# S5 scan and GEGLU on one core: later loads on GpSimd's queue, the fourth token tile after the up weights

## The chip, the cores and the metric

The kernel runs on one core of one Trainium2 chip. The metric is device time in microseconds (us), the median of several executions. Engines are named as in the profile: PE (TensorE, matrix products), PEld (its weight loads), DVE (VectorE), ACT (ScalarE), POOL (GpSimd), SP (SyncE). An engine with a small q (SPq) is its instruction queue; on SP the queue does nothing but issue transfers.

## The reference, cut to what matters

Two branches share a layer norm without weights. Branch A is a diagonal complex state-space scan over 2048 tokens; branch B is a gated feed-forward block.

```python
xn = layernorm(x)                                   # x: 1 x 2048 x 512
# A: P = 512 complex states
dt = exp(log_dt); Lam_bar = exp(dt * Lam)
Bu = einsum("bld,pd->blp", xn, ((Lam_bar - 1) / Lam)[:, None] * Bmat)
for t in range(L): h = Lam_bar * h + Bu[:, t]
s = 2 * einsum("blp,dp->bld", hs, Cmat).real + xn * Dskip
# B: F = 1376
g = silu((gelu(xn @ w_gate) * (xn @ w_up)) @ w_down)
out = x + s * g
```

Inputs and output are bf16.

## The kernel before, in words

The 2048 tokens are worked off in four **slabs** of 512, each slab in four tiles of 128 tokens (tokens on the partitions). `x_tok` holds all tokens. For each slab:

- **norm** (L721 on): statistics of the tokens; for slab 1 on DVE with `bn_stats` (L274), for slabs 2 and 3 on ACT (L738), then the reciprocal root on POOL (L732, L755), and normalised tokens in `xna` on ACT (L743). `dma_t4` (L355) is a transposing DMA from `xna` to `xnT`.
- **B product** (`half`, L528): PE multiplies `xnT` with `BT`, ACT empties the PSUM banks into `U` (L530). DVE turns `U` by a table of angles (`tab`, L540, L548 and L552), runs a real scan per 128 states (L559), and turns back, which gives the states `hst`.
- **gate** (`gate_tile`, L433): the up and gate products in three column chunks of 512, 512 and 352; ACT empties them (L436, Gelu for the gate), DVE multiplies them into `at` (L442, L444). `at_t` (L449) is a transposing DMA from `at` to `atT`, one per tile.
- **down** (`down_pair`, L465): eleven matmuls `atT` by `wd` per tile, Silu on ACT (L468).
- **y** (`y_tile`, L481): states by `C2`; the bank is seeded by ACT with the skip term `sk` (L477), which DVE makes from `xna` and `Drow` (`skip`, L360). DVE multiplies by Silu (L486), adds `x` (L491), and SP stores the tile (L494).

`C2` comes from `CT`, the transposed C matrices. `CT` is the tile `hst1` under another name: two transposing DMAs (L706) write it, ACT multiplies it (L708), DVE combines it (L710, L713), and the second slab's states overwrite it later.

**Slab 0 is special**, since weights are still arriving. Tokens are only centred, not scaled, at first (`center`: sum on ACT L342, subtraction on DVE L343), transposed on PE (`head_t`, L323, copied out by DVE L325), and the root of the variance is put in when the banks are emptied (L391, L407). `squares` (L347, ACT) and `rstd` (L281 to L284, POOL) give that root. `up_rows` (L382) takes the up weight in four row tiles as they land: each row tile is multiplied for token tiles 0 and 1 into six PSUM banks. `first_w` (L401) does the rest of the up products and all gate products of slab 0 with whole columns. PSUM has six `ring` banks and two `ybank` banks.

**Order of work.** Every step is recorded with its engine, and the instructions are emitted in the order of the list `ORDER`, a permutation written out by hand from a planner's run; what the calls give the planner (costs, `rank`, `after`, `not_before`, landing times) is not used when the program is built; only the data steps read and write, and `ORDER`, count. Each engine runs its instructions in that order, and waits only for the data and buffers of its own steps. So an instruction that waits holds all that stand behind it on its engine.

**Queues.** All loads but three tiny ones are issued by SP, in this order: x tiles 0 and 1, up row 0, x tile 2, up row 1, x tile 3, up rows 2 and 3, the gate weight in one (L219, L211), the two B matrices (transposing, L231), slab 0's `xnT` (L355), slab 1's tokens (L214), `wd` without its last 96 rows (L668), Dskip's row to all partitions (L232), then the `atT` transposes, the rest of `wd` (L670), slab 2's tokens, slab 1's `xnT`, the two C matrices (L706), slab 3's tokens. A step on SP waits also for an earlier transfer that used the same completion counter. POOL issues no transfer.

Of the kernel before, what the change touches and what calls it, by code (L numbers as in the profile page):

```python
# [21 lines left out]
    13, 14, 24, 16, 15, 17, 19, 18, 25, 12, 0, 20, 21, 1, 22, 2, 23, 3, 4, 27, 26, 5, 39, 6, 28, 7, 29, 30, 33, 40, 59, 32, 34, 31, 60, 35, 41, 62, 8,  # L22
    61, 48, 63, 9, 67, 36, 42, 49, 56, 43, 44, 37, 65, 64, 45, 68, 50, 51, 66, 57, 52, 69, 70, 47, 46, 10, 71, 54, 72, 82, 58, 53, 136, 138, 74, 55,
    80, 76, 140, 142, 124, 144, 86, 73, 75, 125, 128, 126, 38, 84, 127, 81, 88, 85, 129, 92, 205, 83, 79, 130, 189, 96, 87, 90, 97, 100, 94, 99, 132,
    149, 91, 112, 89, 11, 104, 210, 95, 102, 212, 105, 110, 93, 103, 120, 101, 77, 78, 206, 98, 118, 108, 145, 208, 207, 209, 107, 211, 213, 106, 214,
    113, 116, 109, 146, 155, 117, 215, 137, 151, 115, 139, 143, 150, 157, 119, 111, 121, 122, 123, 141, 153, 158, 219, 131, 148, 154, 170, 172, 217,
    176, 152, 267, 216, 174, 114, 133, 218, 227, 156, 220, 225, 177, 173, 171, 344, 228, 175, 147, 231, 221, 159, 224, 160, 191, 271, 161, 164, 165,
    162, 190, 233, 350, 273, 192, 239, 272, 275, 234, 410, 222, 163, 223, 167, 232, 226, 269, 270, 268, 235, 254, 229, 236, 240, 230, 252, 168, 256,
    193, 169, 166, 178, 255, 253, 257, 237, 250, 290, 286, 251, 194, 195, 238, 274, 284, 288, 179, 276, 180, 277, 287, 291, 292, 294, 305, 301, 183,
    196, 285, 295, 278, 181, 289, 299, 197, 293, 302, 198, 303, 184, 316, 307, 300, 304, 306, 297, 296, 182, 199, 317, 308, 320, 314, 309, 280, 200,  # L30
    201, 321, 186, 310, 315, 322, 318, 202, 282, 323, 203, 187, 319, 324, 335, 329, 279, 325, 281, 312, 188, 204, 331, 337, 333, 326, 185, 327, 134,
    298, 283, 345, 339, 311, 334, 330, 351, 349, 346, 313, 328, 356, 135, 357, 352, 332, 347, 368, 336, 362, 369, 340, 370, 372, 241, 338, 371, 415,
    242, 389, 341, 358, 353, 373, 416, 385, 391, 402, 363, 374, 245, 243, 386, 413, 246, 244, 406, 387, 247, 342, 248, 343, 348, 354, 392, 403, 411,
    375, 407, 457, 412, 417, 249, 258, 388, 404, 429, 408, 431, 430, 418, 390, 414, 405, 259, 263, 261, 419, 435, 444, 409, 260, 359, 420, 432, 262,
    437, 433, 265, 438, 434, 436, 445, 452, 427, 446, 453, 428, 447, 440, 421, 439, 448, 442, 467, 450, 367, 364, 449, 478, 451, 361, 266, 422, 473,
    465, 443, 376, 466, 474, 424, 355, 471, 458, 479, 463, 469, 486, 494, 454, 455, 377, 365, 423, 472, 468, 425, 264, 470, 426, 360, 464, 476, 488,
    490, 456, 495, 487, 381, 484, 492, 489, 491, 475, 366, 477, 480, 459, 485, 499, 379, 380, 496, 515, 517, 481, 378, 500, 482, 493, 497, 460, 382,
    501, 383, 498, 441, 461, 527, 513, 529, 511, 516, 611, 528, 518, 530, 505, 483, 384, 512, 514, 393, 394, 545, 397, 510, 396, 531, 543, 549, 533,
    546, 532, 544, 534, 398, 395, 400, 550, 547, 401, 548, 561, 506, 519, 507, 555, 559, 553, 551, 560, 562, 552, 520, 502, 503, 554, 399, 574, 612,
    522, 557, 576, 566, 556, 613, 558, 614, 521, 577, 575, 567, 568, 570, 508, 579, 563, 509, 581, 569, 571, 582, 616, 524, 583, 572, 617, 573, 523,  # L40
    564, 578, 618, 525, 565, 580, 587, 585, 596, 591, 589, 588, 626, 526, 586, 592, 535, 584, 590, 597, 627, 598, 604, 606, 593, 536, 599, 607, 605,
    621, 602, 600, 540, 594, 622, 633, 631, 601, 595, 615, 619, 603, 537, 608, 609, 620, 610, 539, 462, 623, 538, 634, 541, 635, 636, 628, 542, 624,
    637, 639, 504, 629, 638, 644, 632, 625, 630, 640, 645, 641, 642, 649, 659, 654, 643, 650, 646, 647, 648, 660, 651, 655, 652, 661, 653, 662, 656,
    663, 657, 658,
# [36 lines left out]
def kernel(  # L81
# [17 lines left out]
    nc = tc.nc  # L99
# [113 lines left out]
    def load_slab(s, put, issue, land, **kw):  # L213
        put(issue, land, lambda: nc.sync.dma_start(out=x_tok[:, s * M : (s + 1) * M, :], in_=x_r[:, s * M : (s + 1) * M, :]),  # L214
            writes=[("x", s, m) for m in range(M)], **kw)
# [6 lines left out]
    load_x(1, 1.59, 3.35)  # L222
    load_w("wu", 0, 1, 2.06, 4.6)
    load_x(2, 2.53, 4.95)
    load_w("wu", 1, 2, 3.0, 6.1)
    load_x(3, 3.5, 6.45)
    load_w("wu", 2, 3, 4.0, 7.6)
    load_w("wu", 3, 4, 5.0, 8.8)
    load_w("wg", 0, KT, 6.0, 12.8)
    for ri, src in enumerate((A_B_re, A_B_im)):  # L230
        dma_sp((9.0, 11.5)[ri], (15.3, 17.8)[ri], lambda ri=ri, src=src: nc.sync.dma_start_transpose(out=BT[:, ri, :, :], in_=src), [("BT", ri)])  # L231
    dma(SP, 1.4, 4.9, lambda: nc.sync.dma_start(out=Drow[:], in_=A_Dskip.partition_broadcast(P)), writes=["Drow"], after=list(sp_last))  # L232
# [44 lines left out]
    def rstd(m0, m1):  # L277

        def f():
            if m0 == 0:  # L280
                G.tensor_scalar(out=ve[:, 0:1], in0=mv[:, 0, 1:2], scalar1=EPS, scalar2=None, op0=ALU.add)  # L281
            else:
                G.tensor_scalar(out=ve[:, m0:m1], in0=ss[:, m0:m1], scalar1=1.0 / D, scalar2=EPS, op0=ALU.mult, op1=ALU.add)
            G.tensor_tensor(out=rs[:, 0, m0:m1], in0=ve[:, m0:m1], in1=mhalf[:, m0:m1], op=ALU.pow)  # L284
        pool(0.65 + 0.2 * (m1 - m0), f, [("mv", 0) if m == 0 else ("ss", m) for m in range(m0, m1)] + ["mhalf"], [("rs", 0, m) for m in range(m0, m1)],
             rank=250.0 - 20 * m0)
# [13 lines left out]
    def head_t(m):  # L300
# [17 lines left out]
        bank, key = (ybank[0], ("y", 0)) if m == 1 else (ring[7 - m], ("bank", 7 - m))  # L318
# [27 lines left out]
    def squares(m):  # L346
        acts(512, lambda: act(out=junk()[:], in_=x_tok[:, m, :], func=AF.Square, bias=ma[:, m : m + 1], accum_out=ss[:, m : m + 1]), [("x", 0, m), ("ma", m)], [("ss", m)],  # L347
             ptr=2, rank=150.0 - 10 * m, after=sums0)
# [5 lines left out]
    def dma_t4(s):  # L354
        dma(SP, 2.9 if s < 2 else 1.75, 3.5 if s == 0 else 2.7, lambda: nc.sync.dma_start_transpose(  # L355
            out=xnT[:, s % 2].rearrange("p m k t -> p (m k) t"), in_=xna[:].rearrange("p m d -> p (m d)")),
            [("xn", m) for m in range(M)], [("xnT", s % 2, m) for m in range(M)], rank=20.0)
# [6 lines left out]
    ring_n = [4]  # L364
# [8 lines left out]
    def up_rows(m, k):  # L373

        bs = (0, 1, 2) if m == 0 else ("y0", "y1", 3)
        ps = [ybank[int(r[1])] if isinstance(r, str) else ring[r] for r in bs]
        keys = [("y", int(r[1])) if isinstance(r, str) else ("bank", r) for r in bs]
        ups[m] = list(zip(ps, keys))

        def f():  # L380
            for (a, b), t in zip(CH, ps):
                T.matmul(t[:, 0 : b - a], lhsT=xcT[:, k, m * P : (m + 1) * P], rhs=wu[:, k, a:b], start=(k == 0), stop=(k == KT - 1))  # L382
        pe(3, F // 3, f, [("xcT", m, k // 2), ("wu", k)], keys)
        if k == KT - 1:
            for c in range(3):
                out_up(m, c, *ups[m][c])
# [68 lines left out]
    def down_pair(s, h):  # L455
        gi = g2_n[0] % NG2
        g2_n[0] += 1
        for b in range(2):
# [7 lines left out]
            pe(NFT, 512, f, [("atT", m), "wd"], [("bank", r)])  # L466
# [175 lines left out]
    rstd(1, 2)  # L642
    rstd(2, M)
# [8 lines left out]
    up_rows(1, 2)  # L652
    head_t(3)
    up_rows(0, 3)
    up_rows(1, 3)
    for m in range(2, M):
        for c in range(3):
            first_w("wu", m, c)
    for m in range(M):
        first_gates(m)  # L660
    tables()
# [3 lines left out]
    dma_t4(0)  # L665
    for m in range(M):
        at_t(0, m)
    dma(SP, 0.6, 6.7, lambda: nc.sync.dma_start(out=wd[:, 0 : NFT - 1, :], in_=B_w_down[0 : (NFT - 1) * P, :].rearrange("(k p) d -> p k d", p=P)),  # L668
        reads=[("xnT", 0, 0)], writes=["wd0"], after=list(sp_last))
    dma(SP, 0.5, 4.0, lambda: nc.sync.dma_start(out=wd[:FL, NFT - 1, :], in_=B_w_down[(NFT - 1) * P : F, :]), reads=["wd0"], writes=["wd"])  # L670
# [34 lines left out]
    for ri, src in enumerate((A_C_re, A_C_im)):  # L705
        dma(SP, 2.6, 2.6, lambda ri=ri, src=src: nc.sync.dma_start_transpose(out=CT[:, ri, :, :], in_=src), reads=["wd"], writes=[("CT", ri)])  # L706
# [15 lines left out]
    def norm(s):  # L722
        if s > 1:
            load_slab(s, lambda i, l, e, **kw: dma(SP, i, l, e, **kw), 0.55, 4.0, not_before=30.0)
        else:
            load_slab(1, lambda i, l, e, **kw: dma(SP, i, l, e, after=sp_last[:1], **kw), 0.55, 4.0)
# [93 lines left out]
```

## Time and profile before

| what | value |
|---|---|
| median of 3 runs | 181.9 us (181.57 to 182.25) |
| the profiled execution's own time | 181.37 us |
| its span, first to last instruction | 179.6 us |
| PE busy | 172.4 us, 835 matmuls in the record |
| DVE busy | 155.0 us |
| ACT busy | 126.2 us |
| POOL busy | 11.2 us |
| granted TensorE clock | 1.000 |
| HBM read, written | 6.46 MB, 2.10 MB |

A matmul's end is modelled in the profile, so successive rows overlap; pace is read from start to start. In a timeline a row gives start, length, engine, line, operation, output and inputs, how many were merged, and in brackets how long the engine had been idle and what released it. In the chain of waits a "DMA" piece is the time from a transfer's issue to its landing. "DMA share" is the mean busy share of the core's 16 DMA engines; it can pass 1 where packets overlap.

### The profile page before, as it was taken

The numbers are of one execution on the slowest core, as the hardware profiler recorded it, in microseconds if no ns is written. First come the engines' busy times: TensorE is split into PE (matmuls) and PEld (weight loads), VectorE is DVE, ScalarE is ACT, GpSimd is POOL, SyncE is SP. The second block draws the span as 40 slices with busy tenths as digits, with TensorE's granted clock in tenths as the row PEclk, the third lists the DMA queues.
The fourth block names the chain that finished last, engine by engine and source line by source line (L and its number), as shares of the span: only waits on it lengthen the run. The fifth ranks groups of instructions, "written<-read, shape, count | busy, mean of one in ns | idle before, by whom it ended". The sixth has DMA issues, their size and how long they took to land.

```text
span 179.6 us, 2405 instructions
## 1 busy us (share of the span) xinstructions
PE 172.4 (96%) x835; PEld 82.5 (46%) x850; DVE 155.0 (86%) x252; ACT 126.2 (70%) x240; POOL 11.2 (6%) x23
## 2 busy tenths in 40 slices
PE   7889998999999999999999999999999999999992
PEld 2445543444445554444445544444445445544451
DVE  3658387999999996899999996999999989999663
ACT  5688968999899999995678695658136665561530
POOL 2460003000011000000003000000000000000000
PEclk9999999999999999999999999999999999999999
DMA  5999989899300406900500007973000009045111
GB/s 160 321 295 237 249 276 185 197 220 234 97 0 0 80 0 132 150 0 6 133 0 5 0 0 148 190 148 75 0 0 0 29 30 153 10 98 121 57 61 59
DMA packets 46979, 18.66 MB, mean 104 GB/s; under 512 B 40216, under 2 KB 45944, under 8 KB 46968
## 3 DMA queue, kind: packets, MB, share of 16 engines
q1 hardware_dynamic: 46944, 18.52, 46.6%
q8 instruction: 6, 0.10, 0.2%
q14 instruction: 5, 0.04, 0.1%
q10 hardware_dynamic: 24, 0.00, 0.0%
HBM read 6.46 MB, written 2.10 MB: 48 GB/s over the span
## 4 chain that ended last, share of the span: by engine, by line
PE 81%; DMA 8%; DVE 6%; ACT 2%; issue 1%; SPq 1%; ACTq 0%; DVEq 0%
PE ring L433 31%; PE ring L465 21%; PE ybank L481 14%; PE ring L528 14%; DMA wu<-in_B_w_up_dram 5%; DMA x_tok<-in_A_x_dram 3%; DVE st L274 1%; ACT gt L407 1%; ACT at L391 1%; DVE yg L486 1%; DVE Q L620 1%; DVE tab L620 1%; DVE at L415 1%; DVE ot L491 1%; SPq L219 0%
## 5 line engine op out<-in xcount | busy, mean ns | idle before, releaser
L433 PEld LDWEIGHTS <-xnT 128*128 128x128 bf16 x288 | 28.2, 98 | 28.4
L465 PE MATMUL ring<-wd,atT 128*128 128x512 bf16 (+1 forms) x171 | 39.4, 379 | 0.3
L433 PE MATMUL ring<-wg,xnT 128*128 128x512 bf16 (+1 forms) x142 | 31.5, 356 | 0.1
L433 PE MATMUL ring<-wu,xnT 128*128 128x512 bf16 (+1 forms) x140 | 31.1, 356 | 0.2
L528 PE MATMUL ring<-xnT,BT 128*128 128x512 bf16 x128 | 29.7, 379 | 1.0 <-ACT gt L407 0.8
L559 DVE TENSOR_TENSOR_SCAN Fs<-rho,ini,W 128x512 bf16<-128x512 f32 x24 | 29.9, 1273 | 0.1
L481 PE MATMUL ybank<-C,hst 128*128 128x512 bf16 x118 | 27.4, 379 | 0.1
L465 PEld LDWEIGHTS <-atT 128*128 128x128 bf16 (+1 forms) x176 | 17.2, 98 | 20.8
L436 ACT ACTIVATE gt<-ring 128x512 bf16<-128x512 f32 (+1 forms) x36 | 19.7, 560 | 9.2 <-PE ring L433 9.0
L436 ACT ACTIVATE ub<-ring 128x512 bf16<-128x512 f32 (+1 forms) x36 | 19.1, 559 | 7.8 <-PE ring L433 7.7
L530 ACT ACTIVATE U<-ring 128x512 bf16<-128x512 f32 x32 | 18.1, 598 | 4.9 <-PE ring L528 4.7
L528 PEld LDWEIGHTS <-BT 128*128 128x128 bf16 x128 | 12.5, 98 | 16.5 <-issue 1.8
L481 PEld LDWEIGHTS <-hst 128*128 128x128 bf16 x136 | 13.3, 98 | 13.9
L540 DVE TENSOR_TENSOR Q<-U,tab 128x4096 bf16<-128x4096 bf16 x8 | 18.3, 2290 | 0.3
L540 DVE TENSOR_TENSOR Q<-Fs,tab 128x4096 bf16<-128x4096 bf16 x8 | 18.3, 2286 | 0.1
L468 ACT ACTIVATE g<-ring 128x512 f32<-128x512 f32 x16 | 9.3, 597 | 12.8 <-PE ring L465 12.8
L486 DVE TENSOR_TENSOR yg<-ybank,g 128x512 bf16<-128x512 f32 x15 | 10.2, 686 | 5.4 <-PE ybank L481 3.6
L477 ACT ACTIVATE ybank<-sk 128x512 f32<-128x512 bf16 x15 | 9.0, 601 | 4.4 <-DVE yg L486 4.4
L401 PEld LDWEIGHTS <-W 128*128 128x128 bf16 x72 | 7.0, 98 | 6.8
L442 DVE TENSOR_TENSOR at<-gt,ub 128x1024 bf16<-128x1024 bf16 x12 | 8.2, 683 | 2.2 <-ACT ub L436 1.5
L738 ACT ACTIVATE junk<-x_tok 128x512 bf16<-128x512 bf16 x16 | 10.0, 630 | 0.0
L743 ACT ACTIVATE xna<-x_tok,nb,rs 128x512 bf16<-128x512 bf16 x12 | 9.8, 833 | 0.0
(128 smaller groups left out, 174.1 us busy)
## 6 DMA issues: line engine op xcount, KB each, us to landing
out_dram<-ot SPq DMA_DIRECT2D x15, 128.0 KB, 1.9
x_tok<-in_A_x_dram SPq DMA_DIRECT2D x3, 512.0 KB, 5.1
wu<-in_B_w_up_dram SPq DMA_DIRECT2D x4, 344.0 KB, 4.3
wg<-in_B_w_gate_dram SPq DMA_DIRECT2D x1, 1376.0 KB
wd<-in_B_w_down_dram SPq DMA_DIRECT2D x1, 1280.0 KB, 7.8
x_tok<-in_A_x_dram SPq DMA_DIRECT2D x4, 128.0 KB, 2.6
atT<-at SPq DMA_TRANSPOSE x16, 3.7
Drow<-in_A_Dskip_dram SPq DMA_DIRECT2D x1, 128.0 KB, 7.5
```

The costliest lines, as they stand in the source:

```text
L433: T.matmul(ps[:, 0 : b - a], lhsT=xnT[:, s % 2, m, k, :], rhs=wt[:, k, a:b], start=(k == 0), stop=(k == KT - 1))
L436: acts(b - a, lambda: act(out=dst[:, a:b], in_=ps[:, 0 : b - a], func=AF.Copy if up else AF.Gelu_apprx_tanh), [("bank", r)], [key], table= ...
L465: T.matmul(ps[:], lhsT=atT[:fs, k, m * P : (m + 1) * P], rhs=wd[:fs, k, :], start=(k == 0), stop=(k == NFT - 1))
L468: acts(512, lambda b=b, ps=ps: act(out=g2[gi][:, b, :], in_=ps[:], func=AF.Silu), [("bank", r)], [("g2", gi, b)], table="silu", rank=3.0)
L481: T.matmul(ps, lhsT=hst[s % 2][:, j // NPT, j % NPT, m * P : (m + 1) * P], rhs=C2[:, j // NPT, j % NPT, c0:c1], start=(j == 0 and not seed ...
L486: dve(w, lambda: V.tensor_tensor(out=yg[e][:, c0:c1], in0=ps, in1=g2[gi][:, b, c0:c1], op=ALU.mult), [key, ("g2", gi, b)], [("yg", e, c0)])
L528: T.matmul(ps[:], lhsT=BT[:, ri, k, pt * P : (pt + 1) * P], rhs=xnT[:, s % 2, :, k, :], start=(k == 0), stop=(k == KT - 1))
L530: acts(512, lambda q=q, ri=ri, ps=ps: act(out=U[ui][:, ri, q, :], in_=ps[:], func=AF.Copy), [("bank", r)], [("U", ui, q, ri)])
L540: dve(4096, lambda: V.tensor_tensor(out=Qf, in0=src.unsqueeze(1).to_broadcast(WQ), in1=table, op=ALU.mult), reads, ["Q"], rate=2.0)
L559: pl.add(DVE, 1.12 if s == 0 else 1.185, lambda ri=ri, q=q, pt=pt, first=first: V.tensor_tensor_scan(out=Fs[:, ri, q, :], data0=rho[:, pt ...
L738: acts(512, lambda i=i, fn=fn, sc=sc, m=m: act(out=junk()[:], in_=x_tok[:, s * M + m, :], func=fn, scale=sc, accum_out=sx[:, s, i, m : m + ...
L743: acts(512, lambda m=m: act(out=xn[m], in_=x_tok[:, s * M + m, :], func=AF.Identity, scale=rs[:, s, m : m + 1], bias=nb[:, s, m : m + 1]), ...
```

## The change

- On SP, x tile 3 is issued after up row 3, ahead of the gate weight. `up_rows` gets a third token tile: tile 2's first two column chunks are multiplied row by row too, into banks 4 and 5; its third chunk stays in `first_w`. Tile 2 and 3's transposes use banks 5 and 0.
- Slab 1's tokens, `wd` in its two parts and Dskip's row go to POOL's queue, in that order, after the root of tile 3 (now `rstd` is called for each of the tiles 1, 2 and 3 by itself). Slabs 2 and 3's tokens go to POOL's queue as well.
- The two C transposes on SP follow slab 0's `xnT` directly; they no longer depend on `wd`.
- Squares are planned behind the second sum, not behind all of them.
- `ORDER` is a new permutation of now 667 steps. With it the first gate product of tile 0 (L415) stands ahead of slab 1's statistics on DVE, one gate product of slab 0 stands behind the first two B products on PE, and the y products stand earlier in PE's list (slab 0's first one behind 61.4 us of matmuls instead of 63.2, slab 3's behind 161.5 instead of 163.8), while slab 3's fourth down product stands behind three y products.

Cut to its core (the 25 lines of `ORDER` are left out):

```diff
-            put(issue, land, lambda: nc.sync.dma_start(out=x_tok[:, s * M : (s + 1) * M, :], ...
+            put(issue, land, lambda: G.dma_start(out=x_tok[:, s * M : (s + 1) * M, :], ...
...
     load_x(2, 2.53, 5.1)
     load_w("wu", 1, 2, 3.0, 6.6)
-    load_x(3, 3.5, 6.45)
     load_w("wu", 2, 3, 3.5, 7.7)
     load_w("wu", 3, 4, 4.0, 9.3)
+    load_x(3, 5.0, 9.7)
     load_w("wg", 0, KT, 6.0, 13.3)
...
-    dma(SP, 1.4, 4.9, lambda: nc.sync.dma_start(out=Drow[:], in_=A_Dskip.partition_broadcast(P)), ...
...
-        bank, key = (ybank[0], ("y", 0)) if m == 1 else (ring[7 - m], ("bank", 7 - m))
+        r = 5 if m == 2 else 0
+        bank, key = (ybank[0], ("y", 0)) if m == 1 else (ring[r], ("bank", r))
...
-             ptr=2, rank=150.0 - 10 * m, after=sums0)
+             ptr=2, rank=150.0 - 10 * m, after=sums0[1:2])
...
-        bs = (0, 1, 2) if m == 0 else ("y0", "y1", 3)
+        bs = ((0, 1, 2), ("y0", "y1", 3), (4, 5))[m]
...
-    rstd(1, 2)
-    rstd(2, M)
+    for m in range(1, M):
+        norms = rstd(m, m + 1)
...
+    for k in range(KT - 1):
+        up_rows(2, k)
+    for m in range(3):
+        up_rows(m, KT - 1)
     head_t(3)
-    up_rows(0, 3)
-    up_rows(1, 3)
     for m in range(2, M):
-        for c in range(3):
+        for c in range(2 if m == 2 else 0, 3):
             first_w("wu", m, c)
...
+    late = dma(POOL, 0.9, 5.0, lambda: G.dma_start(out=x_tok[:, M : 2 * M, :], ...), after=[norms])
+    late = dma(POOL, 1.0, 8.0, lambda: G.dma_start(out=wd[:, 0 : NFT - 1, :], ...), writes=["wd0"], after=[late])
+    late = dma(POOL, 0.6, 8.0, lambda: G.dma_start(out=wd[:FL, NFT - 1, :], ...), writes=["wd"], after=[late])
+    dma(POOL, 0.6, 6.0, lambda: G.dma_start(out=Drow[:], in_=A_Dskip.partition_broadcast(P)), ..., after=[late])
...
-    dma(SP, 0.6, 6.7, lambda: nc.sync.dma_start(out=wd[:, 0 : NFT - 1, :], ...), reads=[("xnT", 0, 0)], ...
-    dma(SP, 0.5, 4.0, lambda: nc.sync.dma_start(out=wd[:FL, NFT - 1, :], ...), reads=["wd0"], writes=["wd"])
...
-        dma(SP, 2.6, 2.6, lambda ...: nc.sync.dma_start_transpose(out=CT[:, ri, :, :], in_=src), reads=["wd"], ...
+        dma(SP, 2.6, 2.6, lambda ...: nc.sync.dma_start_transpose(out=CT[:, ri, :, :], in_=src), after=turned, ...
...
-            load_slab(s, lambda i, l, e, **kw: dma(SP, i, l, e, **kw), 0.55, 4.0, not_before=30.0)
+            load_slab(s, lambda i, l, e, **kw: dma(POOL, i, l, e, **kw), 0.9, 5.0, not_before=30.0)
```

In the changed file the lines of the kernel's second half move by a few: L274 becomes L273, L706 and L708 become L711 and L713, L731 and L732 become L735 and L736; L314 to L601 stay or move by one.

## The prediction

> **What bounds the kernel now.** I read the page's busy shares first, then TensorE's (PE's) timeline for its pauses, then the chain of work that ended last, then SyncE's (SP's) timeline and the DMA share by stretch. Shares, from the page:
>
> ```profile
> PE 172.4 (96%) x835; PEld 82.5 (46%) x850; DVE 155.0 (86%) x252; ACT 126.2 (70%) x240; POOL 11.2 (6%) x23
> ```
>
> PE is the bound; the edit removes no matmul (both programs list the same number), so it can only win pauses. PE's timeline (start, us, engine, line, operation, [idle before <- releaser]) holds four, all in the first 34 us:
>
> ```profile
> 6.80 0.59 PE L382 MATMUL ybank<-wu,W 128*128 128x512 bf16 x2 [0.47 <-DMA wu<-in_B_w_up_dram]
> ...
> 7.38 0.39 PE L323 MATMUL ring<-ident,xna 128*128 128x128 bf16 x4
> 7.61 1.32 PE L382 MATMUL ring<-wu,W 128*128 128x512 bf16 x6
> ...
> 10.27 0.74 PE L382 MATMUL ring<-wu,W 128*128 128x512 bf16 x3 [0.54 <-DMA wu<-in_B_w_up_dram]
> ...
> 25.37 2.15 PE L528 MATMUL ring<-xnT,BT 128*128 128x512 bf16 x8
> 28.28 5.63 PE L528 MATMUL ring<-xnT,BT 128*128 128x512 bf16 x24 [0.76 <-ACT gt L407]
> 33.75 7.30 PE L465 MATMUL ring<-wd,atT 128*128 128x512 bf16 x32
> ```
>
> One 512-column matmul is paced at 0.216 us (16 in 3.46 us, chain at 41.04), a 352-column one at 0.149 (4 in 0.60). So the 8 from 25.37 end their pace at 27.10 and PE lost 1.18 us before 28.28 (the row's 0.76 counts from a modelled end); the 24 from 28.28 end at 33.45, and 0.30 more is lost before 33.75. After that PE runs without a pause until the tail. What made the 1.18 is in the chain (start, us, what):
>
> ```profile
> 17.53 0.50 SPq L355
> 18.03 0.04 issue
> 18.07 5.10 DMA x_tok<-in_A_x_dram
> 23.17 0.02 issue
> 23.19 1.88 DVE st L274 x3
> 25.07 0.59 DVE at L415
> ...
> 27.54 1.85 ACT gt L407 x3
> 29.39 0.04 issue
> 29.43 4.48 PE ring L528 x20
> ```
>
> Slab 1's tokens wait in SP's queue behind three transposes until 18.07 and land at 23.17. VectorE (DVE) runs in order and waits 2.85 us for them ahead of tile 0's gate product (L415); that holds the gate buffer, ScalarE's (ACT's) Gelu, and PE's PSUM bank. The DMA's side, in stretches (us; busy of PE, PEld, DVE, ACT, POOL; clock, DMA share, GB/s): three transposes, then plain loads, then one atT transpose alone:
>
> ```profile
> 13.50:20.00 6.50, 6.50 (x37) 3.42 (x35) 5.11 (x13) 5.64 (x10) 0.07 (x1) 1.00 1.12 227
> 20.50:25.50 5.00, 4.95 (x25) 2.41 (x25) 2.31 (x4) 3.89 (x7) 0.00 (x0) 1.00 1.03 341
> 60.25:62.00 1.75, 1.75 (x11) 0.89 (x10) 1.38 (x3) 1.75 (x4) 0.00 (x0) 1.00 1.06 201
> ```
>
> Either kind fills its stretch by itself (share 1.03 to 1.12). They never overlap here: all came from one queue.
>
> **Part 1, x tile 3 behind the last up weight.** wu1's wait ends at 6.80, the one for x tile 3, queued next, at 7.18 (ACT's L342 starts then): 128 KB took 0.38 us. Moved back, it lets the last up row land at 10.23 - 0.38 = 9.85. Before it, PE loses as filler tile 3's four transposes (0.23 by start, 7.38 to 7.61) and gets tile 2's first two products (0.43). Gain 0.38 + 0.20 = 0.58. Tile 3 lands at 10.23; ACT's sum (0.63 + 0.19) ends at 11.05, DVE's centring (0.35) at 11.45. PE has ten matmuls, 2.02 us, from 9.88 to 11.90, so the transposes find their input and their bank (ACT empties bank 0 by 11.7). That cover is 0.2 us thin; were x 0.5 us later, PE would wait 0.3. Bounds from a loss of 0.3 to a gain of 0.58; I take 0.58, since the rows of this very stretch give it.
>
> **Part 2, slab 1's tokens on GpSimd's (POOL's) queue.** The issue stands behind tile 3's reciprocal root. On ACT: sum to 11.05, three evacuations (0.57, 0.57, 0.43 by start), one of tile 2 (0.57), the square (0.90): 14.1. POOL's two (L283, L284, 0.9 together): 15.1, against 18.07. With the row's 5.1 us it lands at 20.2. DVE's new order puts tile 0's gate products ahead of the statistics: I walk DVE to 21.4 there and to 22.1 at the statistics, so neither waits. Next late is tile 1's product, at 25.5 (ACT empties its second y bank then); the Gelu behind it frees bank 2 at 26.7, and PE wants it at 28.2. So the 1.18 and the 0.30 go. The slack is 1.5 us: tokens later than about 23.5 would bring the wait back.
>
> What POOL's six issues cost no row shows: the nearest, SP's plain issues, take 0.42 to 0.93 us. Four of them end by 18.8; behind them stands slab 1's root (L731), ready at 26.9: cost 0. Slabs 2 and 3 follow at about 28.5, and the next root is needed 24 us later.
>
> **Part 3, what SP's queue does now.** The C transposes move from 38.3 to 18.1, behind xnT, and ahead of tile 0's atT transpose: 2.1 and 2.5 us of issue, so SP is free at 22.7, 1.3 after the tile. PE's first product with atT (L465) moves up: 27.15 us of matmuls stand before it in PE's list, 28.87 now. PE now runs 3.4 us behind its list's sum after the head (21.97 us of matmuls before the row at 25.37); less 0.58 that is 2.8, so it wants atT at 29.9. In data time: three transposes 13.5 to 20.2, C 4.2, atT 1.65, landing 0.5: 26.6, hidden by 3.3 us. But wd, slab 1 and Dskip's row (5.5 us, 20.2 to 25.7) now run beside them. If all 16 engines' time adds up, atT lands at 32.1 and PE waits 2.2; if nothing adds, 0. Both kinds show a share over 1 alone, so I sit nearer to the full sum and take three quarters: 30.7, a wait of 0.8. By the same walk ACT comes at 28.0 to its product with C (L713), which stands ahead of bank 0's evacuation; the same lateness pays for both, since PE is waiting then. Dskip's row, last of the four, is wanted by DVE (L360) at 26.9 and lands between 22 and 28; 1 us there is what slab 0's state has to spare at PE (L481), cost 0.
>
> The Trainium skill, "DMA: Bandwidth & Descriptors", section "Issuing engines are not separate DMA queues", speaks against the change: DMAs issued from any engine run on the same 16 DMA engines and interleave. By that rule the sum has the whole 2.2, and 182.0 is the time; no run so far shows the two kinds side by side.
>
> **The rest of the order.** y products move up in PE's list (slab 3's: 161.5 us of matmuls before them, was 163.8). PE is there at 161.5 + 3.0 (2.8 and some instruction refills) = 164.5. DVE's own rows before that state sum to 150.6, so DVE may have lost 13.8 by then. Now it has lost 18 at that place, 10.9 of it in waits after 13.3 (the largest 2.85, 1.63, 1.49, 1.35, 1.25); without the three early ones (2.85, 1.35, 1.25) about 12.5 is left. Cost 0; bounds 0 and the rival below.
>
> **Sum** on the profiled execution (181.37; span 179.6): -0.58 - 1.18 - 0.30 + 0.8 = -1.26, so 180.1. The median of the runs, 181.9, is 0.53 higher; against it 180.64, and I give 180.6.
>
> **Rivals** (times against the median):
> - *Nothing adds up on the DMA engines*: -2.06, 179.8. For: the issue alone takes 1.38 us of an atT transpose's 1.65, so SP might be the limit and the engines have room. Against: the share over 1. 0.16.
> - *All adds up*: -2.06 + 2.2, 182.0, no change. 0.17.
> - *Slower: atT behind everything*. If POOL's queue gets the larger part whenever it has work, slabs 2 and 3 (1 MB, 2.9 us at 360 GB/s) also go before tile 0's atT, which then lands between 32.1 and 35.0. At 33.5 PE waits 3.6: +1.5, 183.4. It decides from an atT landing of 32.9. For: 40,216 of the page's 46,979 packets are under 512 B, nearly all the transposes', so turn by turn the loads would move more. Against: by then POOL's earlier loads are done. 0.20.
> - *Slower: DVE not early*. If DVE's waits come back elsewhere, y of slab 3 starts at 168.3 as before, but 9.3 us of matmuls follow it, not 6.9: +1.5, 183.4. 0.08.
> - *Slower: POOL can't prepare transfers while DVE works.* DVE pauses first at 22.1, so slab 1 lands at 25.3 to 27.3 and wd (7.8 us in its row) near 34: +2, 183.9. Against: POOL's own instructions run beside DVE in this trace (L731 at 26.96 beside L415). 0.05. The Trainium skill, "SBUF — State Buffer", section "Who interferes with whom", has such a lock, but for DVE's two-port modes only; `tensor_tensor`, most of DVE's work there, would be spared, and 0.3 us per scaling (L351) is all that it would cost. No run so far shows such a transfer.
> - *The move does nothing*: POOL's transfer lands as late as SP's did; -0.58 alone, 181.3. 0.02.
>
> **How the numbers follow.** The forecast has 0.32 and covers shares of 0.65 to 0.9 of the 5.5 us (180.1 to 181.4). A measurement of this kernel tells about 0.5% (0.9 us). Faster by more than that: 0.25 of the 0.32, and the 0.16, together 0.41. Within it: the other 0.07, the full sum 0.17, the idle move 0.02, together 0.26. Slower: 0.20 + 0.08 + 0.05 = 0.33. The range 179.6 to 183.4 leaves out the lock and about half of the two at 183.4, 0.19.
>
> **What would show it.** Part 1: PE's wait for wu before about 9.9 under 0.2 us and no new one at tile 3's transposes. Part 2: L273 no longer waiting for x_tok, L528 no longer for ACT. Part 3: whether L465's first matmul waits for a DMA near 30, and the GB/s between 16 and 26 (above 400 would say that the kinds overlap). Wrong would be the forecast if PE pauses again behind 45 us, at L481 on DVE.

## The result, and the profile after

The changed kernel takes 1.0378 times the time of before (95% interval 1.0345 to 1.0412): slower, by some 6.9 us, where 1.3 us of gain had been predicted. Executions that lie far above the others of their kernel (196 to 204 us of the changed one, one of 653 us of sp_all, one of 211 us of act_queue_warm) are left out of the ratios, and the profile read here is that of another execution of the changed kernel, of 187.72 us (span 185.9 us; before 181.37 and 179.6).

From its page, the shares and the granted clock in 40 slices:

```profile
PE 174.2 (94%) x835; PEld 83.1 (45%) x850; DVE 155.7 (84%) x252; ACT 126.3 (68%) x240; POOL 15.8 (8%) x31
...
PEclk9999999969999999999999999999999999999999
```

The matmuls are as many as before; PE's share falls because the span has grown, and one slice shows a lower clock. PE's timeline shows where:

```profile
26.25 1.89 PE L528 MATMUL ring<-xnT,BT 128*128 128x512 bf16 x8 [1.66 <-DMA xnT<-xna]
27.97 1.03 PE L401 MATMUL ring<-wg,W 128*128 128x512 bf16 x4
28.83 3.62 PE L528 MATMUL ring<-xnT,BT 128*128 128x512 bf16 x16
36.92 1.89 PE L465 MATMUL ring<-wd,atT 128*128 128x512 bf16 x4 [4.48 <-DMA atT<-at]
39.03 1.94 PE L465 MATMUL ring<-wd,atT 128*128 128x512 bf16 x6 [0.22 <-issue]
```

The two pauses on ACT's Gelu are gone. In their place PE waits for two DMA transposes: 1.66 us for slab 0's `xnT`, then 4.48 us for tile 0's `atT`. The four matmuls from 36.92 take until 39.03, at 0.53 us each where the pace is 0.2155. The stretches around it (us, then busy of PE, PEld, DVE, ACT, POOL; clock, DMA share, GB/s) say why:

```profile
33.00:36.50 3.50, 0.00 (x0) 0.00 (x0) 0.00 (x0) 0.91 (x1) 0.00 (x0) 1.00 1.17 248
36.60:40.00 3.40, 2.86 (x7) 1.16 (x9) 3.14 (x5) 3.40 (x7) 0.00 (x0) 0.50 0.87 181
40.10:44.00 3.90, 3.90 (x19) 1.76 (x18) 3.80 (x4) 3.19 (x5) 0.00 (x0) 1.00 1.12 208
```

After the long pause the granted clock is 0.50 for 3.4 us. SP's timeline shows what its queue did meanwhile (start, time of the issue):

```profile
16.06 4.31 SPq L355 DMA_TRANSPOSE xnT<-xna  x1
20.41 6.11 SPq L711 DMA_TRANSPOSE hst<-in_A_C_re_dram  x1
26.56 3.35 SPq L711 DMA_TRANSPOSE hst<-in_A_C_im_dram  x1
30.02 10.18 SPq L449 DMA_TRANSPOSE atT<-at  x4
```

The C transposes were to cost 2.1 and 2.5 us of issue and leave SP free at 22.7; they cost 6.11 and 3.35, and it is free at 30.0. The chain that ended last runs through just these:

```profile
18.43 1.94 SPq L355
20.37 0.04 issue
20.41 9.60 DMA hst<-in_A_C_re_dram
30.02 6.86 DMA atT<-at
36.88 0.05 issue
36.92 1.89 PE ring L465 x4
```

And the DMA queues (packets, MB, share of the 16 engines' time) in 22 to 25 us, when GpSimd's first four loads and SP's C transpose had both been issued, and in 31 to 34, when slabs 2 and 3 ran beside `atT`:

```profile
q0 software_dynamic: 246, 1.01, 101.5%
...
q1 hardware_dynamic: 38, 0.00, 1.0%
...
q0 software_dynamic: 254, 0.97, 91.4%
q1 hardware_dynamic: 411, 0.10, 15.2%
```

q0 is GpSimd's queue, q1 SP's. In the first stretch the loads take all of the engines' time and the transposes stand still: by the packet records 29 of SP's 38 packets are the 4-byte ones that close a transfer. In the second SP's 15% all but stop at 31.43 us, just behind the loads' first packet at 31.33. From 31.5 to 33.8 no packet of SP is on record:

```profile
q0 software_dynamic: 219, 0.83, 102.6%
```

Between these two stretches, from 28.1 to 31.3, it is the other way round: SP has 3,372 packets and GpSimd none. So here the two queues take turns in stretches of 2 to 4 us, not packet by packet. The total is 342 and 359 GB/s, little above the 341 of loads alone before.

**The account**, at the start of the first L465. PE's list holds 8 products with B (1.72 us) less ahead of it than before, so before's 33.75 is to be compared as 32.03. The head is 0.08 us faster (PE could start L528 at 17.72 + 6.71 = 24.43; before 25.37, but with 0.86 of gate product ahead of it that now stands behind), the two pauses are gone (-1.48), `xnT` costs 26.25 - 24.43 = 1.82, `atT` 36.92 - 28.83 - 3.45 = 4.64. The sum is +4.9, and 36.92 - 32.03 is 4.89. Halved clock: 4 matmuls in 2.11 us (pace 0.86), 6 in 1.79 (1.29): +1.75. Together +6.6; the span grew by 6.3, and where 0.3 came back isn't traced. ACT waited beside PE: 5.09 us at L713, until 35.59, for the second C transpose.

### The profile page after: what moved, and what is told of

The parts are those of the page before. It is cut to its first block, busy times and chain, and to the rows that moved or that the text cites. A ratio compares the mean times of both kernels' runs of the same rounds, so it can differ in the third digit from the quotient of the medians.

```text
span 194.9 us, 2405 instructions
## 1 busy us (share of the span) xinstructions
PE 176.2 (90%) x835; PEld 83.3 (43%) x850; DVE 155.3 (80%) x252; ACT 126.1 (65%) x240; POOL 16.2 (8%) x31
## 4 chain that ended last, share of the span: by engine, by line
PE 78%; SPq 12%; DMA 3%; DVE 3%; issue 1%; ACT 1%; POOL 1%; ACTq 0%
PE ring L433 28%; PE ring L465 20%; PE ybank L481 13%; PE ring L528 12%; SPq L711 11%; DMA atT<-at 2%; PE ring L382 2%; DMA x_tok<-in_A_x_dram 1%; SPq L355 1%; PE ybank L382 1%; PE ring L481 1%; DVE tab L620 1%; DVE Q L620 1%; ACT junk L347 0%; POOL rs L283 0%
## 5 line engine op out<-in xcount | busy, mean ns | idle before, releaser
L465 PE MATMUL ring<-wd,atT 128*128 128x512 bf16 (+1 forms) x171 | 41.5, 393 | 5.2 <-DMA atT<-at 4.7
L433 PEld LDWEIGHTS <-xnT 128*128 128x128 bf16 x288 | 28.2, 98 | 28.4
L528 PE MATMUL ring<-xnT,BT 128*128 128x512 bf16 x128 | 31.3, 393 | 8.6 <-DMA xnT<-xna 8.6
L530 ACT ACTIVATE U<-ring 128x512 bf16<-128x512 f32 x32 | 18.0, 596 | 23.9 <-PE ring L528 23.8
L433 PE MATMUL ring<-wu,xnT 128*128 128x512 bf16 (+1 forms) x142 | 31.7, 356 | 0.1
L433 PE MATMUL ring<-wg,xnT 128*128 128x512 bf16 (+1 forms) x141 | 31.5, 356 | 0.2
L465 PEld LDWEIGHTS <-atT 128*128 128x128 bf16 (+1 forms) x176 | 17.6, 101 | 27.2 <-DMA atT<-at 5.2
L481 PE MATMUL ybank<-C,hst 128*128 128x512 bf16 x117 | 27.7, 379 | 0.2
L528 PEld LDWEIGHTS <-BT 128*128 128x128 bf16 x128 | 12.8, 101 | 24.7 <-issue 10.9
L481 PEld LDWEIGHTS <-hst 128*128 128x128 bf16 x136 | 13.3, 98 | 14.0
L360 DVE TENSOR_TENSOR sk<-xna,Drow 128x512 bf16<-128x512 bf16 x16 | 6.5, 420 | 7.4 <-DMA Drow<-in_A_Dskip_dram 6.4
L401 PE MATMUL ring<-wg,W 128*128 128x512 bf16 (+1 forms) x47 | 9.7, 356 | 0.1
```

Source lines behind the costliest of these rows:

```text
L401: T.matmul(ps[:, 0 : b - a], lhsT=xcT[:, k, m * P : (m + 1) * P], rhs=wt[:, k, a:b], start=(k == 0), stop=(k == KT - 1))
L433: T.matmul(ps[:, 0 : b - a], lhsT=xnT[:, s % 2, m, k, :], rhs=wt[:, k, a:b], start=(k == 0), stop=(k == KT - 1))
L465: T.matmul(ps[:], lhsT=atT[:fs, k, m * P : (m + 1) * P], rhs=wd[:fs, k, :], start=(k == 0), stop=(k == NFT - 1))
L481: T.matmul(ps, lhsT=hst[s % 2][:, j // NPT, j % NPT, m * P : (m + 1) * P], rhs=C2[:, j // NPT, j % NPT, c0:c1], start=(j == 0 and not seed ...
L528: T.matmul(ps[:], lhsT=BT[:, ri, k, pt * P : (pt + 1) * P], rhs=xnT[:, s % 2, :, k, :], start=(k == 0), stop=(k == KT - 1))
L530: acts(512, lambda q=q, ri=ri, ps=ps: act(out=U[ui][:, ri, q, :], in_=ps[:], func=AF.Copy), [("bank", r)], [("U", ui, q, ri)])
```

## The experiments

Two causes were open: the loads on **GpSimd's queue** (theory: they hold back SP's transposes), and the **C transposes ahead of `atT`** (rival: they alone are late enough). The first four kernels cross them. In `ORDER`, 195 and 196 are the C transposes, 197 to 205 the products with C, 150 slab 0's `xnT`, 154 tile 3's `atT` (the last of slab 0's four), 223 slab 1's `xnT`, 126 to 129 the four late loads, 270 and 413 slabs 2 and 3.

**c_late**: C behind all four `atT` (and 197 to 205 later, too), the loads stay on GpSimd.

```diff
-    ..., 138, 91, 195, 196, 99, ...
-    ..., 139, 154, 413, 270, ...
+    ..., 138, 91, 99, ...
+    ..., 139, 154, 195, 196, 413, 270, ...
```

> The changed kernel with the two C transposes moved back on SyncE's queue behind tile 3's atT transpose (and the three first products with C a little later on ScalarE and VectorE); the loads stay on GpSimd's queue. Theory 'turns': the 16 DMA engines take turns between the two queues packet by packet, 4096 B of a load against 256 B of a transpose, so the xnT transpose of slab 0 crawls while GpSimd's queue has work: it still lands after 28 us, PE still waits 6 to 9 us for it at L528, only the second pause at L465 gets shorter (1 to 3 us instead of 4.7); 184 to 190 us. Rival 'order': the C transposes ahead of atT are the harm; then xnT lands near 20.5, both pauses go, 179 to 182 us.

1.0421 (1.035 to 1.0492). PE's timeline:

```profile
26.77 1.89 PE L528 MATMUL ring<-xnT,BT 128*128 128x512 bf16 x8 [2.33 <-DMA xnT<-xna]
...
46.73 4.85 PE L465 MATMUL ring<-wd,atT 128*128 128x512 bf16 x11 [4.89 <-ACT U L530]
```

`atT` is no longer waited for, while `xnT` still is, with no C transpose near it: that wait belongs to GpSimd's queue (6 to 9 us of it had been expected). The 4.89 us are of my making: ACT's product with C (L713) stood ahead of evacuations in ACT's list and its input now came later. So its time does not price the order of C.

**sp_c_early**: all six loads on SP, C still ahead of `atT`. `wd`, its rest, Dskip's row, and slabs 2 and 3 are changed like slab 1; 126 to 129 stand behind 150, 413 behind 223.

```diff
-    late = dma(POOL, 0.9, 5.0, lambda: G.dma_start(out=x_tok[...
+    late = dma(POOL, 0.9, 5.0, lambda: nc.sync.dma_start(out=x_tok[...
```

> The changed kernel with the six loads issued on SyncE's queue (slab 1, wd, its rest and Dskip's row right behind slab 0's xnT transpose, slabs 2 and 3 around slab 1's xnT), the C transposes still ahead of tile 0's atT. Theory 'turns': with one queue nothing takes turns; xnT lands near 20.5, no pause at the first L528; the data of 5.5 us of loads and 4.2 us of C transposes then stand ahead of atT, which lands near 32.5 against 29.9, so PE waits 2 to 3 us at L465: 181 to 183 us. Rival 'order': 187 us or more, as the changed kernel.

1.0229 (1.0159 to 1.0299). SP's and PE's timelines:

```profile
22.57 5.73 SPq L711 DMA_TRANSPOSE hst<-in_A_C_re_dram  x1
28.34 2.30 SPq L711 DMA_TRANSPOSE hst<-in_A_C_im_dram  x1
30.74 7.12 SPq L449 DMA_TRANSPOSE atT<-at  x4
```

```profile
25.12 1.89 PE L528 MATMUL ring<-xnT,BT 128*128 128x512 bf16 x8
26.85 1.03 PE L401 MATMUL ring<-wg,W 128*128 128x512 bf16 x4
27.71 3.62 PE L528 MATMUL ring<-xnT,BT 128*128 128x512 bf16 x16
34.84 1.89 PE L465 MATMUL ring<-wd,atT 128*128 128x512 bf16 x4 [3.51 <-DMA atT<-at]
```

Without GpSimd's queue the wait for `xnT` is gone. The C transposes then stand behind 5.5 us of loads in SP's own queue, `atT` behind both, and PE waits 3.51 us for it (and the clock is 0.50 from 34.4 to 37.9). So the order alone is late enough for a long wait; both theories hold a part. The time, 186.7 us, lies above the 181 to 183 of the one theory, just under the 187 of the other.

**sp_c_late**: both edits.

> Both of the two together: all loads on SyncE's queue, and the C transposes behind tile 3's atT. Both theories: no pause over 1 us behind 12 us; 179 to 181 us. If it still stands at 184 or more, neither the second queue nor the C transposes are the cause, and the lists of the other engines are to be looked at.

1.0281 (1.018 to 1.0382). No wait for a DMA at L528 or L465, but 4.43 us at L465 on ACT's U (L530): ACT waited 5.43 us at L713 for the C transpose, ahead of the evacuation:

```profile
39.84 1.15 ACT L713 ACTIVATE tF<-hst,cim 128x1024 f32<-128x1024 bf16 x1 [5.43 <-DMA hst<-in_A_C_im_dram]
```

My placing again, so this doesn't yet say that the pair explains all.

**act_queue**: the changed order, its six loads (five places) issued by ACT.

```diff
-    ... lambda: G.dma_start(
+    ... lambda: nc.scalar.dma_start(
```

> The changed kernel with the same six loads issued by ScalarE, on its hardware queue, at the places where GpSimd's stand in the order. Theory 'turns': any second queue takes turns; its packets are 1024 B (as these loads' packets are in the kernel before), so transposes get about a fifth of the bytes instead of a seventeenth: xnT lands at 23 to 25, PE waits up to 2 us there; 181 to 185 us. Rival 'software': the crawl comes from GpSimd's preparing of transfers; then xnT lands near 20.5 to 21.5, and the time is 180 to 182 us. Either way ScalarE pays 0.4 to 0.9 us for each issue.

1.0253 (1.0168 to 1.0339). The queues from 19 to 21 us, q10 being ACT's:

```profile
q10 hardware_dynamic: 539, 0.55, 80.4%
q1 hardware_dynamic: 539, 0.14, 31.7%
```

Packet for packet, 1,024 bytes against 256: the loads get the larger part, yet the transposes go on. `xnT` still comes late, and nothing waits at L465:

```profile
29.01 3.17 PE L528 MATMUL ring<-xnT,BT 128*128 128x512 bf16 x8 [4.27 <-DMA xnT<-xna]
```

That is longer than the 1.66 us behind GpSimd's loads, and the time is above what both theories gave. ACT issued slab 1's load at 13.44 us, 2 us ahead of GpSimd, so the two waits don't compare the queues alone. But a second queue that isn't GpSimd's holds `xnT` up as well. The Trainium skill, "DMA: Bandwidth & Descriptors", section "Queues, rings and completion order", says that each DMA engine takes turns between the queues that have work, packet by packet. If the profile's packets are the page's, these 539 to 539 agree; GpSimd's 246 to 38 in the changed kernel do not.

**sp_all**: all on SP; C behind slab 1's `xnT`, its products later, slab 2 behind `atT`.

```diff
-    ..., 228, 180, 178, 223, 230, ...
+    ..., 228, 180, 178, 223, 195, 196, 413, 230, ...
```

> The changed kernel with all six loads on SyncE's queue (slab 1, wd, its rest, Dskip's row behind slab 0's xnT; slab 2 behind the atT transposes, slab 3 behind the C transposes), the C transposes behind slab 1's xnT, and the products with C later on ScalarE and VectorE, near where the kernel before has them, so that nothing waits for C. Theory 'turns' (two queues side by side starve the transposes): no pause over 1 us behind 12 us, 179.5 to 181.5 us. Rival 'lists' (the new order of PE's, ScalarE's and VectorE's work is itself worse): 184 us or more.

1.0139 (1.0085 to 1.0192). Its three siblings put one thing each back on GpSimd's queue.

**slab1_pool**: slab 1 there (126 at its old place).

> As the one with all loads on SyncE, but slab 1's 512 KB on GpSimd's queue at the place of the change (near 15.3 us). 'Turns': 128 packets of 4096 B, about 2 us of the engines, hold slab 0's xnT transpose back by as much, to 22.5; PE wants it near 24.3, so nothing is lost: 179.5 to 181.5 us. Rival 'any use of GpSimd's queue beside transposes is dear': xnT lands after 25 and the time is over 183 us.

1.0162 (1.0091 to 1.0232): no different from sp_all. Its profile shows what it still lost: PE waits 4.0 us at L433 for ACT, as DVE waited 4.2 for ACT's product with C (L713). My placing of 197 to 205 once more. sp_all has no profile of an execution that its ratio counts; that it lost the same is borne out by sp_all2 alone.

**wd_pool**: `wd`, its rest and Dskip's row there.

> As the one with all loads on SyncE, but wd, its rest and Dskip's row (1.5 MB) on GpSimd's queue at the places of the change. 'Turns': about 4.5 us of loads run while slab 0's xnT stands in the other queue; xnT lands at 25 to 29, PE waits 1 to 5 us at L528, and where the pause is over 2 us the granted clock is halved for 3.4 or 6.8 us behind it (another 1 to 3 us): 182 to 188 us. Rival 'slabs 2 and 3 or slab 1 are the harm': 179.5 to 181.5 us.

189.6 to 199.2 us, too far apart for a ratio; every one is above all those of sp_all that the ratio counts (184.4 to 184.8). So `wd` on that queue is costly even with C late.

**slabs23_pool**: slabs 2 and 3 there.

> As the one with all loads on SyncE, but slabs 2 and 3 (1 MB) on GpSimd's queue behind slab 1's root, near 28 us. 'Turns': they run from 29 to 33 beside tile 1's to tile 3's atT transposes, which PE wants from about 33 on; PE waits 0 to 3 us at L465: 180 to 184 us. Rival 'only what runs beside xnT matters': 179.5 to 181.5 us.

1.0192 (1.0141 to 1.0244), with 0.6 us of wait for `atT`: by the medians 0.7 us above sp_all, inside the intervals.

**sp_all2**: sp_all with the first products with C earlier.

```diff
-    ..., 257, 256, 275, ..., 254, 197, 198, 199, 287, ..., 295, 292, 200, 201, 202, 305, ...
+    ..., 257, 256, 197, 198, 199, 275, ..., 254, 200, 287, ..., 295, 292, 201, 202, 305, ...
```

> The kernel with all six loads on SyncE once more, its first two products with C placed earlier on ScalarE (the first near 47 us, the second near 50.5), so that VectorE does not wait 4.2 us for the first one and PE not 4.0 us behind 50 us, as the profile of the one with slab 1 on GpSimd showed. 'Turns': that profile's 182.7 us span less 4.0 us is 178.7, 180.5 us in time: 179.5 to 181.5. Rival 'lists': still 183.5 or more, with another wait in place of the 4.0 us.

1.0007 (0.998 to 1.0035): all the harm is gone, and so is the gain. PE's timeline, what PE waited for (us in total, times, longest), and the stretch of 49 to 73 us:

```profile
23.87 1.89 PE L528 MATMUL ring<-xnT,BT 128*128 128x512 bf16 x8
25.59 1.03 PE L401 MATMUL ring<-wg,W 128*128 128x512 bf16 x4
26.46 3.62 PE L528 MATMUL ring<-xnT,BT 128*128 128x512 bf16 x16
29.91 2.54 PE L465 MATMUL ring<-wd,atT 128*128 128x512 bf16 x11
```

```profile
PE ring L433 <- ACT ub L436: 0.9, 3, 0.5
...
PE ring L433 <- ACT gt L436: 0.3, 1, 0.3
```

```profile
49.00:73.00 24.00, 22.70 (x110) 10.47 (x109) 21.69 (x44) 23.36 (x39) 1.01 (x1) 1.00 0.20 21
```

The first L465 starts at 29.91; before's comparable 32.03 makes that 2.1 us earlier, just the 2.06 of the prediction's first two parts. Then PE's rows from 48.9 to 74.1, start to start against the pace, lose 0.25, 0.12, 0.66, 0.40, 0.35 and 0.46: 2.2 us, 1.2 of it marked as waits for ACT. ACT is busy 23.36 of these 24 us. The same stretch of before:

```profile
49.00:73.00 24.00, 23.90 (x121) 11.84 (x121) 21.05 (x35) 23.16 (x38) 1.31 (x1) 1.00 0.26 50
```

There ACT was as full, and PE just did not wait for it. What PE had gained ahead of this stretch it gave back in it.

**slab1_pool2**: the same with slab 1 on GpSimd.

> The same with slab 1's 512 KB on GpSimd's queue where the change has it. 'Turns': xnT is held back to about 24.2, when PE wants it (0.5 us of wait in the run before this one): 179.5 to 181.8 us, within 0.5 us of the kernel with all loads on SyncE. Rival 'any use of GpSimd's queue beside transposes is dear': over 1.5 us slower than it.

1.001 (0.9983 to 1.0037). The change's most direct part costs nothing and gains nothing. `xnT`'s closing packets come at 23.2 us instead of sp_all2's 20.6, still ahead of PE's first L528 at 23.96.

**act_queue_warm**: act_queue with 18 matmuls on constants while PE waits for `xnT`, into the bank that the next product then overwrites. It asks whether the halved clock has a price of its own.

```diff
+                    for _ in range(warm_n.pop() if warm_n else 0):
+                        T.matmul(ps[:], lhsT=warm[:, 0:P], rhs=warm, start=True, stop=True)
                     for k in range(KT):
```

> The kernel with the loads on ScalarE's queue, with 18 matmuls of 512 columns on constants (3.9 us, their result is overwritten) put into PE's list right ahead of the first L528, to fill its 4.3 us pause there. Theory 'the pause also costs the clock': the granted clock stays at 1.0 where it was 0.5 from 29.45 to 32.87, the eight and four matmuls there take 2.8 us instead of 4.7, and the time falls by 1.5 to 2 us from 186.7 to about 185. Rival 'the clock has nothing to do with the pause': 186.5 to 187, or later by what the fillers delay.

1.0208 (1.0153 to 1.0264), against 1.0253: 185.04 to 186.80 us with a mean granted clock of 1.00, act_queue 186.07 to 188.57 with 0.978 to 0.987. That is 1.7 us by the medians of the executions counted (185.05 and 186.71) and 0.8 by the ratios, but the intervals overlap; the direction fits, the size isn't shown.

**sp_all3**: sp_all2 with the first product with C one place earlier still, the second behind two Gelus, to give ACT room.

```diff
-    ..., 273, 274, 243, 172, ..., 256, 197, 198, ..., 254, 200, 287, ...
+    ..., 273, 274, 243, 197, 172, ..., 256, 198, ..., 254, 287, ..., 292, 200, 201, ...
```

> All loads on SyncE's queue; the first product with C one place earlier on ScalarE (near 45 us, where it idles 0.9 us), the second behind two Gelus (near 55 us) instead of ahead of the evacuations at 51. In the run before it PE lost 1.5 us between 49 and 73 us in waits for ScalarE (0.25, 0.50, 0.23, 0.19, 0.29), which gave back what the head had won. Theory: the first two go: 0.4 to 0.8 us less than that run, 181.2 to 181.8 against 181.95 of the kernel before, a ratio of 0.995 to 1.000. Rival: ScalarE is full in that stretch whatever the place, and the waits only move: 1.000 to 1.003.

1.0024 (1.0001 to 1.0048). PE still waits for ACT at L433, 1.3 us in all: the waits moved and did not go, as the rival had it. That no other order would do better isn't shown.

**wd_split**: wd_pool with `wd` in four loads of 128 columns, meant to make GpSimd's packets 256 bytes.

```diff
-    lambda: G.dma_start(out=wd[:, 0 : NFT - 1, :], ...
+    lambda: [G.dma_start(out=wd[:, 0 : NFT - 1, c : c + P], ...) for c in range(0, D, P)]
```

> The kernel with wd, its rest and Dskip's row on GpSimd's queue, wd now as four loads of 128 columns (rows of 256 B instead of 1024 B). Theory 'turns by packet': if the packets of GpSimd's queue become 256 B, the transposes get half of the bytes instead of a seventeenth and PE's wait at the first L528 falls from 6.8 to 1 to 4 us; the loads themselves take longer. If the trace still shows packets of 4096 B, the wait stays at 5 us or more and the run tells nothing of packet size. Rival 'the queue of GpSimd blocks SyncE's whatever its packets': packets of 256 B and still 5 us or more.

1.0642 (1.0582 to 1.0701), and L528 waits 4.23 us for `xnT`. The packet records show GpSimd's packets still at 4,096 bytes, so the question (does the packet's size decide who goes first?) wasn't put. What it does show: with C late, `wd` on that queue makes the kernel 6% slower than before, where sp_all, the same order with all on SP, is 1.4% slower.

**after_again**: the changed kernel, for the profile above.

> The changed kernel itself. Its first profile is of an execution of 196.7 us, 7.8 us longer than the executions that the comparison uses. If this profile is of a shorter one, theory 'turns' expects the same two pauses, at the first L528 (xnT) and at the first L465 (atT), both shorter, 5 to 9 us together instead of 13.3, and one stretch of halved clock instead of two. Rival: the shorter executions lose their 7 us elsewhere.

187.72 us, beside 181.48 of the kernel before on that chip. The two waits are 6.1 us together, within the 5 to 9 expected, with one stretch of halved clock.

## Why the prediction was wrong, by its own steps

**Part 1** (-0.58): right in size where up row 1 lands in time. With no wait for `wu` (sp_all2) L528 starts at 23.87, 0.64 earlier than before's 25.37 less the 0.86 of the moved product. But that wait was 0.40 in the changed kernel (gain 0.08) and 1.42 in sp_c_early (a loss of 0.6): the transfers at the start vary by more than the term. (The prediction's "27.15 ... 28.87 now" is the changed list first and the one of before second.)

**Part 2** (-1.18 and -0.30): right. GpSimd issued slab 1's load at 15.45 (15.1 predicted), DVE's statistics ran from 22.3 without a wait for it, and both of PE's pauses on ACT's Gelu were gone in every kernel with the new order and no late DMA.

**Part 3** (+0.8): **the step that failed**, "I sit nearer to the full sum and take three quarters: 30.7, a wait of 0.8". `atT` landed at 36.9, and the wait was 4.5. Four things were wrong in it.
- That the kinds hardly overlap was right: 342 and 359 GB/s, where over 400 would have spoken against it. But the sum was shared out as if evenly, over the loads of 20.2 to 25.7 alone. While GpSimd's loads ran the transposes stood still (38 packets against 246, then none against 219), and slabs 2 and 3, which the sum left out, went ahead of `atT` too. Even the full sum with slabs 2 and 3, which the rival has at 35.0, is 1.9 us short.
- It started the damage behind `xnT`. `xnT` itself landed at 26.2, and PE waited for it: +1.82 that no term held. In the packet records its 2,048 data packets went from 19.05 to 22.10 us, but the 32 closing 4-byte packets only at 23.76 to 25.51; with all on SP they are done at 20.6 (sp_all2). The same section of the Trainium skill's "DMA: Bandwidth & Descriptors" says that the write that signals the end lands only behind every earlier write of that DMA engine, those of other queues too. That fits these records; no run here isolates it.
- On one queue, too, C and the loads ahead of `atT` cost more than the full sum's 2.2 us: 3.51 (sp_c_early).
- A pause of that length is not only its length: the clock behind it, +1.75, was not priced.

**The rest of the order** (0): right as to L481, where PE did not wait behind 45 us. Not right that nothing is late next: with the harm undone, the 2 us go again at L433, where PE waits for ACT between 49 and 73 us (sp_all2, sp_all3).

**The rivals.** "atT behind everything" was the mechanism that came, down to slabs 2 and 3 passing it (31 to 34 us). Its price (+1.5, 183.4) was too small: it took `atT` at 33.5 and left out `xnT` and the clock. "Nothing adds up" and "all adds up" both fell to the sharing. "POOL can't prepare" and "the move does nothing" fell with slab 1's packets, which ran from 17.12 to 20.18 while DVE worked, and "DVE not early" with PE not waiting at L481. (That rival's 168.3 for the start of slab 3's y is 169.0 in before's rows.)

**What each half costs** doesn't add up: all on SP with C late 1.0007, on SP with C early 1.0229, the changed kernel 1.0378, GpSimd's `wd` with C late 1.0642 (in four pieces, and with the late products with C that cost sp_all its 1.0139).

**Open**: why GpSimd's queue gets more than its turn (the order of closing packets is argued, not shown; packet size untested). The bytes can't be all of it: in another profiled execution of the changed kernel, of 196.67 us, the same two waits are 8.59 and 4.73 us, and from 23.25 to 27 us, with `xnT` still out, both queues together move 52 GB/s; in act_queue it is 8 GB/s from 22.75 to 24. Open is also whether some order of ACT's work keeps the 2 us. No version beat before: 1.0007, 1.001 and 1.0024 are the best.

## What to carry to other kernels

Before a load goes to another queue, list what stands in the first queue beside it, and price each of those transfers as late by all of the load, the one in flight too. A transfer that PE waits for is moved behind nothing that can wait. And before a pause is counted as gain, look for the next stretch in which another engine is as full as PE: here ACT, busy 23.2 us of 24 in the profile of before, had given warning that the gain might not last.

## What the runs showed of the hardware

- A load on GpSimd's queue beside SP's DMA transposes held them almost still (246 to 38 packets in 3 us, 219 to none in 2.3); one on ACT's queue took turns (539 to 539).
- SP's issue of one transpose stretched from 2.0 to 2.5 us to 6.11 behind GpSimd's loads, and to 5.73 behind SP's own (sp_c_early): a price for an issue read from an idle queue doesn't hold on a full one.
- The granted clock stayed at 1.00 after pauses of PE of 1.66 and 2.33 us, and was 0.50 after those of 3.51, 4.23, 4.27, 4.43 and 4.48, for 3.4 us each; after 4.73, 4.89, 6.84 and 8.59 for 6.8. Pauses of 2.56 us fall on both sides: 3.4 us at 0.50 in wd_pool and wd_split, none in slabs23_pool. The Trainium skill, "TensorE: Matmul & The Clock Gate", section "Why this matters for your kernels", warns of idle gaps over some 3 us; the two of 2.56 were shorter and still halved the clock.

```profile
72.90 3.44 PE L433 MATMUL ring<-wu,xnT 128*128 128x512 bf16 x9 [2.56 <-ACT ub L436]
```

```profile
73.00:76.00 3.00, 3.00 (x9) 1.19 (x9) 2.96 (x7) 2.96 (x6) 0.00 (x0) 0.50 0.00 0
```

- The clock records explain that. In all traces with a change ahead of the tail, the changes lie whole multiples of 3.413 us apart (3.413 and 30.72 in the changed kernel, 6.83 and 37.55 in wd_pool). With PE's rows laid over that grid, every piece of 3.41 us in which PE was busy for 1.36 us or less was followed by one at 0.50 (the fullest of them: wd_split, 67.03 to 70.44), and no piece at full clock with 1.41 us or more was (the emptiest: slab1_pool, 61.64 to 65.05, with a pause of 2.57). c_late's second piece at 0.50 followed one at 0.50 with more work in it. So what counted was how a pause lay on the grid, not its length alone.
- GpSimd's loads went in packets of 4,096 bytes even where each row piece was 256 (wd_split).
